# Second chunk's scores issued ahead of its global scores, shifted values behind the casts, first FFN steps interleaved by tile

## The chip, the cores and the metric

The kernel runs on one NeuronCore of a Trainium2 chip. A core has five engines with a queue each, worked off in order: TensorE (PE, matrix products; PEld is its weight load), VectorE (DVE), ScalarE (ACT), GpSimd (POOL) and SyncE (SP), which here only issues DMAs. TensorE writes to PSUM, eight banks of 2 KB in each of 128 partitions; VectorE and ScalarE read it from there. Semaphores make an engine wait for another. The metric is the device time of one execution in microseconds, lower is better.

## What is computed

Sparse attention over 8 batches, 8 heads, 576 positions and 64 dimensions, with a window of 32 to each side and 8 global positions, followed by a gated feed-forward block (FFN):

```python
mask = np.abs(pos[:, None] - pos[None, :]) <= window
mask = mask | is_global[:, None] | is_global[None, :]
attn = softmax(np.where(mask, scale * q @ k.T, -1e9))
x = (attn @ v).transpose(0, 2, 1, 3).reshape(4608, 512)
g, val = x @ w_gate, x @ w_val
ffn_out = (gelu(g) * val) @ w_out
out = x + sigmoid(x @ w_res) * ffn_out
```

Inputs and output are float32; the products run in bfloat16. q, k and v are random, the global positions are drawn at random too.

## The kernel before, in words

The 4608 tokens are worked in nine chunks of 512, each of eight windows of 64 tokens (a batch has nine windows). A chunk goes through attention and then through the FFN: twelve steps `ffn_in` (two products of 512 columns, g_ps and v_ps; Gelu on ScalarE; a product on VectorE into ht) and four times `ffn_out`, one for each tile of 128 tokens: a gate (r_ps, then tanh into rsb) and three thirds of four matmuls into f_ps, the last followed by prb on VectorE, ob on GpSimd and the store on SP's queue. The order of all instructions is written out by hand: each engine gets them in the order of the program, and the loop puts the attention of chunk c + 1 between the gates and thirds of chunk c.

Attention of a chunk has these pieces. `scores(c, quad)` makes the windowed scores of four windows in four PSUM banks, called sc: heads 0 to 3 (pp = 0) in two banks of the pool pss, heads 4 to 7 (pp = 1) in two of the pool psm; for the second chunk ScalarE's exp is written back to the bank, and the returned `mask` multiplies it by maskw on VectorE into pt. `global_scores(b)` makes the global rows and columns of batch b: sg, 288 columns in each of the two banks of the pool psn, and ss, 320 columns in a bank of pss. `global_exp` (L481) takes the exp of both, into ptg and gt, and multiplies gt by maskr on VectorE. `global_rows` (L488) makes the values of the global rows, sn, and vgs from it. `local_values` (L551) and `values` (L567) then make the attention output of one tile of 128 tokens in two banks, nd: 16 products with pt, two or four with gt and vgs, then rden and xtok on VectorE. `turn_x` (L591) transposes xtok on TensorE (tx) and copies it to xt, the operand of the FFN.

PSUM pools are rings: psm has four banks (g_ps, v_ps, r_ps, f_ps, half of sc), pss two (the other half of sc, ss, transposes), psn one pair (sg, nd, from the third batch on also sn). A new tile waits until the one that had its place has been read.

Values are held twice: ve for windows that start at an even multiple of 64, vo shifted by half a tile for odd ones. For batch 1, the casts from float32 to ve and the copies from ve to vo (`shift_on_chip`, L106, two copies for each n) are on GpSimd, in its queue between the casts of the staged weight pieces (L145), which come over SP's queue. Chunk 1 has windows 8 of batch 0 and 0 to 6 of batch 1, so its tiles 1, 2 and 3 read vo at n = 0, 1 and 2.

The first chunk's FFN is begun tile by tile: `begin(t)` (L756) issues the four products of steps j = 0 and 1 for the 128 tokens of tile t. The place between the first chunk's FFN and the second chunk's attention is written out on its own, at L852 to L893.

Of the kernel before, what the change touches and what calls it, by code (L numbers as in the profile page):

```python
# [8 lines left out]
F32 = mybir.dt.float32  # L9
# [3 lines left out]
ACTF = mybir.ActivationFunctionType  # L13
# [10 lines left out]
def kernel(  # L24
# [12 lines left out]
    nc = tc.nc  # L37
# [4 lines left out]
    SCALE = 1.0 / float(D) ** 0.5  # L42
# [15 lines left out]
    psm = ctx.enter_context(tc.tile_pool(name="psm", bufs=4, space=bass.MemoryType.PSUM))  # L58
# [44 lines left out]
        eng.dma_start(vo[b % 2][0:64, 0:4, :, :], ve[b % 2][64:128, 0:4, :, :])  # L103
        eng.dma_start(vo[b % 2][64:128, 0:4, :, :], ve[b % 2][0:64, 1:5, :, :])

    def shift_on_chip(n):  # L106
        nc.gpsimd.tensor_copy(vo[1][64:128, n:n + 1, :, :], ve[1][0:64, n + 1:n + 2, :, :])
        nc.gpsimd.tensor_copy(vo[1][0:64, n:n + 1, :, :], ve[1][64:128, n:n + 1, :, :])


    def flat32(t, o):
# [356 lines left out]
    def global_scores(b):  # L468
        sg = psn.tile([128, 2, 512], F32, name="sg", tag="nd")
        for hf in range(2):  # L470
            for p in range(NP):
                nc.tensor.matmul(sg[32 * p:32 * p + 32, hf, 0:288], kgz[b % 2][:, p, :],  # L472
                                 qt[b % 2][:, p, 288 * hf:288 * hf + 288], start=True, stop=True)
        ss = pss.tile([128, 5, 64], F32, name="ss", tag="sc")
        for c in range(5):
            for p in range(NP):
                nc.tensor.matmul(ss[:, c, 16 * p:16 * p + 16], kt[b % 2][:, p, 128 * c:128 * c + 128],  # L477
                                 qgz[b % 2][:, p, :], start=True, stop=True)
        return sg, ss

    def global_exp(b, sg, ss):  # L481
        e = b % 2
        nc.scalar.activation(ptg[e], ss, ACTF.Exp, bias=0.0, scale=SCALE)
        g = gt[e][:, 64:64 + S]
        nc.scalar.activation(g.rearrange("p (a c) -> p a c", a=2), sg[:, :, 0:288], ACTF.Exp, bias=0.0, scale=SCALE)
        nc.vector.tensor_tensor(g, g, maskr, ALU.mult)

    def global_rows(b):  # L488

        e = b % 2  # L490
        if b > 1:
            sn = psn.tile([128, 2, 512], F32, name="sn", tag="nd")[:, 0, 0:2 * VG]
        else:
            sn = pss.tile([128, 2 * VG], F32, name="sn", tag="sc")
        for c in range(-1, 5):
            for p in range(NP):
                if c < 0:
                    nc.tensor.matmul(sn[32 * p:32 * p + 32, :], own[e][:, 32 * p:32 * p + 32],
                                     view(vgb, 0, 128, (b // 2) * VG, [[0, 2], [1, VG]]), start=True, stop=False)
                else:  # L500
                    nc.tensor.matmul(sn[32 * p:32 * p + 16, :], ptg[e][:, c, 16 * p:16 * p + 16],
                                     ve[e][:, c, 2 * p:2 * p + 2, :], start=False, stop=(c == 4))
        nc.vector.tensor_tensor(view(vgs, 0, 128, e * H * VG, [[2 * VG, NP], [VG, 2], [1, VG]]),
                                view(sn, 0, 128, 0, [[0, NP], [VG, 2], [1, VG]]),
                                view(head8, 0, 128, 0, [[2, NP], [1, 2], [0, VG]]), ALU.mult)
# [24 lines left out]
        nc.scalar.activation(sc if stay else mine, sc, ACTF.Exp, bias=0.0, scale=SCALE)  # L530
        return mine, sc if stay else mine

    def scores(c, quad):

        i0 = (CH * c + 4 * quad) % NW
        banks = []
        for pp, pool, tag in ((0, pss, "sc"), (1, psm, "mm")):
            sc = [pool.tile([128, 2, 4, 64], F32, name="sc", tag=tag) for _ in range(2)]
            heads(c, quad, pp, sc, True)
            banks += [(pp, u, sc[u]) for u in range(2)]  # L540
        mine = [weigh(quad, *which, stay=(c == 1)) for which in banks]

        def mask(n0, n1):
            for m, x in mine[n0:n1]:
                nc.vector.tensor_tensor(m, x, view(maskw, 0, 128, 64 * i0, [[0, 2], [64, 4], [1, 64]]), ALU.mult)  # L545
        return mask
# [206 lines left out]
    values(0, 1, begun_v[1])  # L753
    begun = [ffn_steps(0, j) for j in range(2)]

    def begin(t):  # L756
        for steps in begun:
            for what in "gv":
                steps[what](128 * t, 128 * t + 128)

    values(0, 2)
    turn_x(0, 0)
    begin(0)
    values(0, 3)
    turn_x(0, 1)
    begin(1)
    turn_x(0, 2)
    turn_x(0, 3)
    begin(2)
    begin(3)  # L770
# [8 lines left out]
    for c in range(NCH):  # L779
# [8 lines left out]
        for j in range(NFF):  # L788
            if c or j > 1:
                ffn_in(c, j, turns.get(j) if c == 0 else None)  # L790
            if c == 0:
                if j == 0:
                    mask_rows(0, NW)
                elif j == 1:
                    mask_rows(NW, NWM)
                    zero_k(1)
                elif j == 2:
                    zero_gt(1, nc.vector)
                    zero_globals(1)
                    for n in range(1, B // 2):  # L800
                        nc.vector.tensor_single_scalar(idx[:, n:n + 1], idx[:, 0:1], float(2 * H * S * n), ALU.add)
                elif j == 3:
                    zero_v(1, nc.vector)
                elif j == 4:
                    double_qk(0, 1)
                elif j == 6:
                    got = turn_globals(0, 1)
                    for what in "kq":
                        DVE(compact[what][:, 0:1, :], got[what])
                    spread_qk(1, compact, 0, {"k": DVE, "q": ACT})  # L810
                elif j == 5:
                    for p in (0, 1, 2, 3, -1):
                        for what in "kq":
                            cast_pair(1, p, what, POOL)
                    load_vraw(1)
                    for n in (14, 15):
                        load_piece(n)
                    for n in (12, 13):
                        cast_piece(n, POOL)
                    for n in range(16, 20):  # L820
                        load_piece(n)
                    for c5 in range(5):
                        cast_v(1, c5, POOL)
                        if c5 in (1, 2):
                            shift_on_chip(c5 - 1)
                    for n in range(14, 20):
                        cast_piece(n, POOL)
                        if n == 15:
                            shift_on_chip(2)
                    shift_on_chip(3)  # L830
                if j == 10:
                    turn(3)
            elif b < B:
                if c % 2 == 1:
                    n0, n1 = b // 2, b // 2 + 1
                    if j == 8:
                        double_qk(n0, n1)
                    elif j == 9:
                        got = turn_globals(n0, n1)
                        for what in "kq":  # L840
                            DVE(compact[what][:, n0:n1, :], got[what])
                        spread_v(n0, n1)
                if j == 8:
                    shift_v(b)
                    if b + 1 < B:
                        load_qk(b + 1)
                if j == 9:
                    spread_qk(b, compact, (b // 2) * 128, {"k": DVE, "q": DVE})
                if j == 11:
                    held = global_scores(b)  # L850
        work_f = [w for t in range(4) for w in ffn_out(c, t)]
        if c == 0:  # L852
            def third(t, n):
                work_f[4 * t + 1 + n]()

            global_exp(1, *global_scores(1))
            work_f[0]()
            scores(1, 0)(0, 4)
            work_f[4]()
            work_f[8]()  # L860
            mask = scores(1, 1)
            mask(0, 2)
            work_f[12]()
            global_rows(1)
            mask(2, 4)
            for what in "kq":
                load_second(what)
            cast_second("k", 0, NQT, ACT)
            began = local_values(1, 0)
            third(0, 0)  # L870
            values(1, 0, began)
            third(1, 0)
            values(1, 1)
            third(2, 0)
            turn_x(1, 0)
            third(3, 0)
            values(1, 2)
            turn_x(1, 1)
            third(0, 1)
            cast_second("q", 0, 1, POOL)  # L880
            values(1, 3)
            third(1, 1)
            cast_second("q", 1, 3, POOL)
            turn_x(1, 2)
            third(2, 1)
            third(3, 1)
            turn_x(1, 3)
            for t in range(4):
                third(t, 2)
                if t == 1:  # L890
                    cast_second("q", 3, NQT, POOL)
                    turn_qk(2, "k")
            continue  # L893
# [50 lines left out]
```

## Time and profile before

| | us |
|---|---|
| median of 4 runs | 397.74 |
| lowest and highest | 396.79, 398.22 |
| the profiled execution | 398.05 |
| its span | 396.3 |
| TensorE busy | 380.6 |
| VectorE busy | 203.8 |
| GpSimd busy | 170.9 |
| ScalarE busy | 168.2 |
| TensorE busy from 23.00 to 31.35 us (8.35) | 6.27 |
| TensorE busy from 51.31 to 65.09 us (13.78) | 12.40 |

The span is the time from the first to the last instruction of the program in the trace; the profiled execution's own time holds what lies around it too. Times of events below are counted from the span's start. [...]two neighbours overlap by about 0.16 us, and a group of four with 512 columns, shown as 1.02 to 1.04 us, is followed by the next after 0.86. The granted TensorE clock was 1.00 throughout.

### The profile page before, as it was taken

Reading aid. Unit: us, or ns where it says so; the run is one execution under the profiler, and the core shown is the slowest. Engines: PE = TensorE matmul, PEld = TensorE weight load, DVE = VectorE, ACT = ScalarE, POOL = GpSimd, SP = SyncE. Lnnn points to the kernel's source line nnn. Section 1 sums busy time; section 2 is a strip of 40 time slices with the busy share of each in tenths; the row PEclk is TensorE's granted clock in tenths of the full one; section 3 lists DMA queues with packets and bytes.
Section 4 is the critical chain, followed back from the end, with each engine's and each line's share of the span. In section 5 each row is a group of like instructions: output and inputs, shape, how many; then the busy total and the mean of one; then the engine's idle time right before and its main releaser. Section 6 shows DMA issues by size and latency. Waiting matters only on the chain.

```text
span 396.3 us, 8484 instructions
## 1 busy us (share of the span) xinstructions
PE 380.6 (96%) x3360; PEld 197.1 (50%) x3360; DVE 203.8 (51%) x445; ACT 168.2 (42%) x279; POOL 170.9 (43%) x207
## 2 busy tenths in 40 slices
PE   3979989999999999999999999999999999999996
PEld 2665546444554454445544554455445544554444
DVE  7766676446733464456444554565345633463423
ACT  5653585136333542355334623373336333633321
POOL 7977794768247614471395226612501110021012
PEclk9999999999999999999999999999999999999999
DMA  8999999399939962999299949993990310051002
GB/s 249 268 379 348 231 348 195 97 164 171 97 108 144 190 70 80 127 197 101 79 132 158 140 82 108 184 101 84 116 152 19 94 55 0 2 92 57 0 29 79
DMA packets 153002, 52.78 MB, mean 133 GB/s; under 512 B 136386, under 2 KB 143426, under 8 KB 152962
## 3 DMA queue, kind: packets, MB, share of 16 engines
q1 hardware_dynamic: 77024, 41.88, 46.1%
q0 software_dynamic: 75392, 9.84, 41.4%
q8 instruction: 26, 0.43, 0.5%
q10 hardware_dynamic: 546, 0.52, 0.4%
q14 instruction: 14, 0.11, 0.1%
HBM read 39.19 MB, written 9.44 MB: 123 GB/s over the span
## 4 chain that ended last, share of the span: by engine, by line
PE 85%; DVE 5%; DMA 3%; ACT 2%; issue 2%; POOL 2%; DVEq 0%; POOLq 0%
PE f_ps L661 21%; PE g_ps L618 21%; PE v_ps L618 21%; PE r_ps L636 7%; PE nd L563 4%; PE sc L523 3%; PE nd L575 2%; DMA kt<-k_st 2%; DMA vgf<-in_v_dram,idx 1%; PE ss L477 1%; POOL ve L99 1%; DVE pt L545 1%; PE sg L472 1%; PE sc L512 1%; PE tx L598 1%
## 5 line engine op out<-in xcount | busy, mean ns | idle before, releaser
L625 DVE SCALAR_TENSOR_TENSOR ht<-gsb,v_ps 128x512 bf16<-128x512 bf16 x108 | 74.1, 687 | 98.9 <-PE v_ps L618 91.5
L624 ACT ACTIVATE gsb<-g_ps 128x512 bf16<-128x512 f32 x108 | 64.4, 597 | 126.3 <-PE g_ps L618 126.3
L667 POOL TENSOR_TENSOR ob<-prb,xtok 128x512 f32<-128x512 f32 x35 | 40.3, 1155 | 175.8 <-DVE prb L665 175.8
L618 PE MATMUL g_ps<-xt,wg_t 128*128 128x512 bf16 (+1 forms) x456 | 111.9, 368 | 1.8 <-ACT xt L599 1.8
L618 PE MATMUL v_ps<-xt,wv_t 128*128 128x512 bf16 (+1 forms) x456 | 111.9, 368 | 0.1
L661 PE MATMUL f_ps<-wo_t,ht 128*128 128x512 bf16 x420 | 100.4, 379 | 0.0
L618 PEld LDWEIGHTS <-wg_t 128*128 128x128 bf16 x456 | 43.4, 98 | 51.2 <-issue 2.9
L618 PEld LDWEIGHTS <-wv_t 128*128 128x128 bf16 x456 | 43.4, 98 | 49.4 <-DVE xtok L582 0.3
L661 PEld LDWEIGHTS <-ht 128*128 128x128 bf16 x420 | 38.8, 97 | 38.5
L639 ACT ACTIVATE rsb<-r_ps 128x512 bf16<-128x512 f32 x36 | 21.6, 604 | 71.0 <-PE r_ps L636 71.0
L665 DVE SCALAR_TENSOR_TENSOR prb<-rsb,f_ps 128x512 f32<-128x512 bf16 x35 | 24.0, 685 | 27.4 <-PE f_ps L661 26.4
L636 PE MATMUL r_ps<-wr_t,xt 128*128 128x512 bf16 x144 | 36.8, 379 | 0.0
L530 ACT ACTIVATE pt<-sc 128x512 bf16<-128x512 f32 x64 | 33.3, 614 | 5.2 <-PE sc L523 5.2
L91 POOL DMA_DIRECT2D q_st<-in_q_dram x25 | 21.4, 865 | 21.1 <-DMA qt<-q_st 21.0
L545 DVE TENSOR_TENSOR pt<-pt,maskw 128x512 bf16<-128x512 bf16 x56 | 23.2, 424 | 7.8 <-ACT pt L530 5.8
L563 PEld LDWEIGHTS <-pt 128*128 128x128 bf16 x576 | 21.9, 97 | 8.5 <-DVE xtok L588 1.2
L99 POOL DMA_DIRECT2D ve<-in_v_dram x30 | 25.5, 864 | 0.0
L588 DVE TENSOR_TENSOR xtok<-nd,rden 128x512 bf16<-128x512 f32 x34 | 23.5, 691 | 1.3
L91 POOL DMA_DIRECT2D k_st<-in_k_dram x25 | 21.1, 868 | 4.0 <-DMA kt<-k_st 2.3
L587 DVE RECIPROCAL rden<-nd 128x8 f32<-128x8 f32 x34 | 7.1, 207 | 30.4 <-PE nd L575 30.3
L563 PE MATMUL nd<-ve,pt 128*128 128x65 bf16 x320 | 22.5, 193 | 0.0
L636 PEld LDWEIGHTS <-xt 128*128 128x128 bf16 x144 | 13.4, 97 | 15.0
(168 smaller groups left out, 308.7 us busy)
## 6 DMA issues: line engine op xcount, KB each, us to landing
out_dram<-ob SPq DMA_DIRECT2D x35, 256.0 KB, 2.2
vo<-ve SPq DMA_DIRECT2D x12, 260.0 KB, 5.8
q_st<-in_q_dram POOLq DMA_DIRECT2D x20, 128.0 KB, 6.1
k_st<-in_k_dram POOLq DMA_DIRECT2D x20, 128.0 KB, 6.3
ve<-in_v_dram POOLq DMA_DIRECT2D x18, 128.0 KB, 6.9
wo_t<-in_k_dram SPq DMA_DIRECT2D x8, 256.0 KB, 6.2
vraw<-in_q_dram SPq DMA_DIRECT2D x8, 256.0 KB, 7.5
extra<-in_moe_w_out_dram SPq DMA_DIRECT2D x4, 512.0 KB, 7.3
```

The lines of the kernel that those rows point to most:

```text
L91: nc.gpsimd.dma_start(dst[0:n, r, :].rearrange("p (h d) -> p h d", d=D), src[b].rearrange("h s d -> s h d")[128 * r:128 * r + n])
L99: nc.gpsimd.dma_start(t[p0:p1, c, :, 0:D], v[b].rearrange("h s d -> s h d")[s0 + p0:s0 + p1])
L530: nc.scalar.activation(sc if stay else mine, sc, ACTF.Exp, bias=0.0, scale=SCALE)
L545: nc.vector.tensor_tensor(m, x, view(maskw, 0, 128, 64 * i0, [[0, 2], [64, 4], [1, 64]]), ALU.mult)
L563: nc.tensor.matmul(nds[h // 4][:, VG * (h % 4):VG * (h % 4) + VG], view(pt, 0, 128, c0, [[1, 128]]), vw, start=(h % 4 == 0 and e == 0), st ...
L618: nc.tensor.matmul(held[what][:, c0:c1], w[:, kk, 128 * j:128 * j + 128], x[:, kk, c0:c1], start=(kk == 0), stop=(kk == NKT - 1))
L624: nc.scalar.activation(gsb, held["g"], ACTF.Gelu, bias=0.0, scale=1.0)
L625: nc.vector.scalar_tensor_tensor(ht[:, j, :], gsb, 0.5, held["v"], ALU.mult, ALU.mult)
L636: nc.tensor.matmul(r_ps, xt[c % 2][:, kk, 128 * t:128 * t + 128], wr_t[:, kk, :], start=(kk == 0), stop=(kk == NKT - 1))
L661: nc.tensor.matmul(held["f"], ht[:, j, 128 * t:128 * t + 128], wo_t[:, j, :], start=(j == 0), stop=(j == NFF - 1))
L665: nc.vector.scalar_tensor_tensor(prb, held["r"], 1.0, held["f"], ALU.add, ALU.mult)
L667: nc.gpsimd.tensor_tensor(ob, prb, xtok[c % 2][:, t, :], ALU.add)
```

## The change

Four things are changed. The first steps of the FFN are put in another order among the attention tiles and transposes. For the second chunk, the scores of heads 0 to 3 are issued before the global scores, and the masks are split in the same way; ss goes into the columns of sg's two banks that are free (288 to 480 of the first, 288 to 416 of the second), so that its exp is two instructions; sn takes psn's pair for batch 1 as well. The value products of the second chunk's first tile follow vgs and stand ahead of the first third. And the four shifts of batch 1's values stand behind its casts: n = 0 on GpSimd behind the last v cast, n = 3 behind the last weight cast, n = 1 and 2 on ScalarE behind the last gate.

```diff
-    def shift_on_chip(n):
-        nc.gpsimd.tensor_copy(vo[1][64:128, n:n + 1, :, :], ve[1][0:64, n + 1:n + 2, :, :])
-        nc.gpsimd.tensor_copy(vo[1][0:64, n:n + 1, :, :], ve[1][64:128, n:n + 1, :, :])
+    def shift_on_chip(n, copy):
+        copy(vo[1][64:128, n:n + 1, :, :], ve[1][0:64, n + 1:n + 2, :, :])
+        copy(vo[1][0:64, n:n + 1, :, :], ve[1][64:128, n:n + 1, :, :])
...
-        ss = pss.tile([128, 5, 64], F32, name="ss", tag="sc")
+        if b == 1:
+            ss = [sg[:, c // 3, 288 + 64 * (c % 3):352 + 64 * (c % 3)] for c in range(5)]
+        else:
+            ss_all = pss.tile([128, 5, 64], F32, name="ss", tag="sc")
+            ss = [ss_all[:, c, :] for c in range(5)]
...
     def global_exp(b, sg, ss):
         e = b % 2
-        nc.scalar.activation(ptg[e], ss, ACTF.Exp, bias=0.0, scale=SCALE)
+        to = ptg[e].rearrange("k c r -> k (c r)")
+        done = 0
+        for part in ss:
+            n = part.shape[1]
+            nc.scalar.activation(to[:, done:done + n], part, ACTF.Exp, bias=0.0, scale=SCALE)
+            done += n
...
     def global_rows(b):
...
-        if b > 1:
+        if b:
             sn = psn.tile([128, 2, 512], F32, name="sn", tag="nd")[:, 0, 0:2 * VG]
...
-    def scores(c, quad):
+    def scores(c, quad, pps=(0, 1)):
...
-        for pp, pool, tag in ((0, pss, "sc"), (1, psm, "mm")):
+        for pp in pps:
+            pool, tag = (psm, "mm") if pp else (pss, "sc")
...
-    def begin(t):
-        for steps in begun:
+    def begin(t, js=(0, 1)):
+        for j in js:
             for what in "gv":
-                steps[what](128 * t, 128 * t + 128)
+                begun[j][what](128 * t, 128 * t + 128)
 
     values(0, 2)
     turn_x(0, 0)
-    begin(0)
     values(0, 3)
     turn_x(0, 1)
+    begin(0, (0,))
+    turn_x(0, 2)
+    begin(0, (1,))
     begin(1)
-    turn_x(0, 2)
     turn_x(0, 3)
     begin(2)
     begin(3)
...
                     for c5 in range(5):
                         cast_v(1, c5, POOL)
-                        if c5 in (1, 2):
-                            shift_on_chip(c5 - 1)
+                    shift_on_chip(0, POOL)
                     for n in range(14, 20):
                         cast_piece(n, POOL)
-                        if n == 15:
-                            shift_on_chip(2)
-                    shift_on_chip(3)
+                    shift_on_chip(3, POOL)
...
-            global_exp(1, *global_scores(1))
+            scores(1, 0, (0,))(0, 2)
+            got = global_scores(1)
+            scores(1, 0, (1,))(0, 2)
+            global_exp(1, *got)
             work_f[0]()
-            scores(1, 0)(0, 4)
             work_f[4]()
+            scores(1, 1, (0,))(0, 2)
             work_f[8]()
-            mask = scores(1, 1)
-            mask(0, 2)
+            mask = scores(1, 1, (1,))
             work_f[12]()
             global_rows(1)
-            mask(2, 4)
+            mask(0, 2)
+            for n in (1, 2):
+                shift_on_chip(n, ACT)
             for what in "kq":
                 load_second(what)
             cast_second("k", 0, NQT, ACT)
-            began = local_values(1, 0)
+            values(1, 0)
             third(0, 0)
-            values(1, 0, began)
+            values(1, 1)
             third(1, 0)
-            values(1, 1)
             third(2, 0)
```

`work_f` holds the gates at 0, 4, 8 and 12 and the thirds between them; `third(t, n)` issues third n of tile t.

More of the change, by code (lines that the diff above doesn't have):

```diff
@@ L473, in global_scores @@
                                  qt[b % 2][:, p, 288 * hf:288 * hf + 288], start=True, stop=True)
-        ss = pss.tile([128, 5, 64], F32, name="ss", tag="sc")
+        if b == 1:
[3 more added lines that the diff above has]
+            ss = [ss_all[:, c, :] for c in range(5)]
         for c in range(5):
             for p in range(NP):
-                nc.tensor.matmul(ss[:, c, 16 * p:16 * p + 16], kt[b % 2][:, p, 128 * c:128 * c + 128],
+                nc.tensor.matmul(ss[c][:, 16 * p:16 * p + 16], kt[b % 2][:, p, 128 * c:128 * c + 128],
                                  qgz[b % 2][:, p, :], start=True, stop=True)
-        return sg, ss
+        return sg, [sg[:, 0, 288:480], sg[:, 1, 288:416]] if b == 1 else [ss_all.rearrange("k c r -> k (c r)")]
     def global_exp(b, sg, ss):
         e = b % 2
-        nc.scalar.activation(ptg[e], ss, ACTF.Exp, bias=0.0, scale=SCALE)
+        to = ptg[e].rearrange("k c r -> k (c r)")
[4 more added lines that the diff above has]
+            done += n
         g = gt[e][:, 64:64 + S]
```

## The prediction

> **What bounds the kernel now.** I read the page first (busy shares and the chain that ended last), then TensorE's timeline where the chain leaves TensorE, then VectorE's and ScalarE's timelines there, last the DMA landings that feed GpSimd.
>
> ```profile
> PE 380.6 (96%) x3360; PEld 197.1 (50%) x3360; DVE 203.8 (51%) x445; ACT 168.2 (42%) x279; POOL 170.9 (43%) x207
> PE 85%; DVE 5%; DMA 3%; ACT 2%; issue 2%; POOL 2%; DVEq 0%; POOLq 0%
> ```
>
> TensorE is the bound: time can be won only where it stands. From 75 to 380 us it hardly does (windows: 20.00 busy of 20.00, 20.00 of 20.00, 264.20 of 265.00). The change touches two stretches before that. The first, at 23 to 31 us, starts the FFN tile by tile (TensorE's timeline: start, duration, line, work, idle before and its releaser):
>
> ```profile
> 23.10 0.69 PE L598 MATMUL tx<-ident,xtok 128*128 128x128 bf16 x4
> 24.46 0.38 PE L618 MATMUL g_ps<-xt,wg_t 128*128 128x128 bf16 x4 [0.67 <-ACT xt L599]
> 25.44 0.40 PE L618 MATMUL v_ps<-xt,wv_t 128*128 128x128 bf16 x4
> 26.38 0.38 PE L598 MATMUL tx<-ident,xtok 128*128 128x128 bf16 x4
> 27.44 0.38 PE L618 MATMUL g_ps<-xt,wg_t 128*128 128x128 bf16 x4 [0.67 <-ACT xt L599]
> 28.33 0.61 PE L598 MATMUL tx<-ident,xtok 128*128 128x128 bf16 x8
> 29.39 0.38 PE L618 MATMUL g_ps<-xt,wg_t 128*128 128x128 bf16 x4 [0.45 <-ACT xt L599]
> 31.35 1.02 PE L618 MATMUL g_ps<-xt,wg_t 128*128 128x512 bf16 x4
> ```
>
> Each turn (tx) is followed at once by the product that needs its copy, so TensorE waits for the copy three times. The second, 51.3 to 65.1 us, goes from the first chunk's FFN to the second chunk's attention (TensorE, then VectorE, then ScalarE):
>
> ```profile
> 53.72 0.62 PE L523 MATMUL sc<-qt,kt 64*128 64x64 bf16 x31 [0.38 <-ACT ptg L483]
> 56.97 0.42 PE L523 MATMUL sc<-qt,kt 64*128 64x64 bf16 x16 [0.41 <-DVE pt L545]
> 59.87 1.02 PE L661 MATMUL f_ps<-wo_t,ht 128*128 128x512 bf16 x4
> 62.42 0.20 PE L563 MATMUL nd<-vo,pt 128*128 128x65 bf16 x1 [0.22 <-DVE xtok L588]
> ```
>
> ```profile
> 54.24 1.48 DVE L486 TENSOR_TENSOR gt<-gt,maskr 128x576 bf16<-128x576 bf16 x1 [1.60 <-ACT gt L485]
> 55.64 3.81 DVE L545 TENSOR_TENSOR pt<-sc,maskw 128x512 bf16<-128x512 f32 x6
> 59.49 0.70 DVE L503 TENSOR_TENSOR vgs<-sn,head 128x520 bf16<-128x520 f32 x1
> 60.10 1.28 DVE L545 TENSOR_TENSOR pt<-sc,maskw 128x512 bf16<-128x512 f32 x2
> ```
>
> ```profile
> 51.94 1.28 ACT L483 ACT_TABLE_LOAD   x1
> 54.57 2.08 ACT L530 ACTIVATE sc<-sc 128x512 f32<-128x512 f32 x4
> ```
>
> VectorE has no gap from 54.24 to 62.36, ScalarE none from 51.3 to 60.1; TensorE's work in these 13.78 us, at its own pitches (four full 512-column matmuls 0.864, 16 score matmuls 0.29, a value tile 0.49), is 11.45, so it loses 2.3.
>
> [...] The trace shows 1.28 and the exp directly behind it (53.23)[...]; I take 1.28. [...] the gt product took 1.48 beside GpSimd's casts, and 0.46 at 97.34 us, when GpSimd only issued DMAs.
>
> **Part 1, first steps interleaved (gain).** The new order is turn 0, values tile 3, turn 1, steps of tile 0 for j=0, turn 2, those for j=1, tile 1, turn 3, tiles 2 and 3. Work is the same; I walk it with the trace's times. Turn 0's last matmuls go at 23.5 and it ends issuing at 23.7. Values tile 3 uses the pair of banks that tile 1 frees when VectorE's xtok ends at 24.29: start 24.35, 0.49 + 0.22, end 25.06. Turn 1 to 25.28. j=0 for tile 0 (copy ready 24.42) 0.44, to 25.72. Turn 2 (xtok ends 25.38) to 25.94. j=1 0.44, to 26.38 (its bank, free at 25.38, no longer stops it). Tile 1 (ScalarE's copy 25.5 to 26.1) 0.89, to 27.28. Turn 3 (xtok for tile 3: VectorE free at 25.38, 0.2 + 0.7, ends 26.3) to 27.50. Tile 2 (copy 26.1 to 26.7) to 28.39, tile 3 (VectorE's copy ends 28.1) to 29.28. Before it was 31.17 (30.95 + 0.22). Gain 1.89, between 1.5 (a copy late once more, 0.4) and 2.0 (all the idle there is). Cover lost: none; the FFN steps behind it need weight casts that end at 24.9 (j=2, needed at 29.5), 30.3 (j=4, needed 33) and 35.8 (j=8, needed 40).
>
> **Part 2, scores first, shared banks (cost).** Times of the trace before, moved by nothing; part 1 is subtracted at the end. TensorE: first two score banks 51.4 to 51.7 (the slots come free at 50.93 and 51.30 with the kt and qt copies), sg and ss to 52.6, two more score banks to 52.9, first two gates to 54.65. ScalarE loads its table as before, 51.94 to 53.22; the load now carries waits for TensorE and VectorE, both over by 51.9. Then four exps at 0.49, to 55.2; two ptg parts of 192 and 128 columns instead of one of 320 (0.44)[...]; gt exp to 56.2; two gates to 57.2; exps of the second half to 58.1; gate; exps to 59.55; last gate 60.1. VectorE: four masks at 0.635 from 53.78 to 56.3; gt product to 57.8 if blocked like before, 56.8 if not; I take blocked, though it matters little, since mask five needs ScalarE at 57.6; masks five and six to 59.0; vgs to 59.7; the last two masks to 60.9; rden and xtok to 61.9, against 62.36 before. TensorE waits 0.4 for the third pair of score banks, 0.35 for gate three, 0.2 and 0.2 after (banks held by masks and gates); then sn 58.3 to 58.7. Now the loss: sn, sg and the value tiles share one pair of banks. The first value tile cannot start until vgs has read sn, 59.77: 1.03 idle, where before the tile ran early and the first output third (0.86) lay behind it. Then tile 0 to 60.71, third to 61.57, tile 1 waits for xtok until 61.94 and ends 62.65; thirds 1, 2, turn, third 3 (2.80) end at 65.46. Before: 65.09. So VectorE's 0.45 is won and 0.86 of work is put behind it: cost 0.37. Bounds: gain 0.5 if the gt product is short and banks come free a little earlier[...].
>
> **Part 3, shifted values (nothing).** GpSimd loses four copies (0.65 each, 2.6) ahead of its last v cast, but that cast's data lands at 51.14 (landings from the DMA issues), so it ends near 51.8 instead of 53.45; sn needs it at 58.3 - 1.89 = 56.4, and did not wait before. The out weights land at 52.36 to 60.42; the last cast ends near 61.6 as before, the thirds that need it start near 69. ScalarE's four copies (1.06 for twice the size at 20.8 us; 0.55 each) run at 60.1 to 62.3, on the shifted clock 58.2 to 60.4; behind them in its queue are the k_st casts, whose data lands at 61.5 to 65.8. The DMAs on SP's queue (second k and q loads) hang on the same casts and stay. GpSimd's q casts stand ahead of the first outputs: the third q row lands at 69.33, its cast ends 70.0, the first output now comes at 71.1. TensorE would be held there only from a shift of about 3.5. Price if the cover failed: 0.4, the copy that values tile 2 needs.
>
> **Sum.** -1.89 + 0.37 = -1.52. The profiled execution took 398.05 (span 396.3), so 396.5; the median of the runs, 397.74, is 0.3 below it, so 396.2.
>
> **Rivals.** (B) The second stretch gains too: banks freed earlier because masks start at 53.78 instead of 55.64, gt product short, so -0.5 there: -2.4, 395.3. For: VectorE idles 1.6 before its gt product now. Against: ScalarE has no gap, and the last exps cannot come earlier. (C) The shared pair costs more than worked: vgs 1.0 later, so -0.5, 397.2. For: it hangs on ScalarE's order (gates ahead of exps five and six)[...]. Against: each hand-over was timed above. (D) Slower: [...] the product beside a later cast of GpSimd (up to 1.04 more); TensorE has nothing in front of the first value tile, so each microsecond on vgs is one on the end. It decides from vgs later than 61.2 (1.52 beyond 59.7)[...]. For: no cover is left. [...]
>
> **How the numbers follow.** A 0.50 (its own range 395.5 to 396.9), B 0.18, C 0.23, D 0.09. A measurement of this kernel tells 0.3% (1.2 us) from no change. Faster by more: 0.8 of A, all of B, a little of C: 0.60. Slower: most of D, 0.08. Within: 0.32. The range takes in B and most of C: 394.9 to 397.6.
>
> **What would show it.** Right: the first 512-column g_ps starts near 29.5; idle before the first value tile of the second chunk near 1 us, released by vgs; all later stages the same length. Wrong: first g_ps after 30; that value tile released otherwise; idle between 65 and 95 us, where nothing is foreseen.

## The result and the profile after

The changed kernel took 396.66 us (median of 42 runs, 395.28 to 400.56), the kernel before 397.73 (63 runs, 395.96 to 400.58): 1.07 us less, a ratio of 0.9971 with a 95% interval of 0.9961 to 0.9981. The profiled execution took 395.56 us, its span is 393.9. That is 2.4 us under the span before, more than the medians differ, because one execution also carries chance: in this one the first transpose of the first chunk came at 22.17 us instead of 23.10, from code that the change leaves alone, and over the fourteen profiles of this study it came anywhere from 22.07 to 23.28.

The page's first part, busy time by engine:

```profile
PE 379.9 (96%) x3360; PEld 196.8 (50%) x3360; DVE 202.3 (51%) x445; ACT 170.7 (43%) x284; POOL 168.6 (43%) x203
```

TensorE is as busy as before. ScalarE's busy time rose by 2.5 us, for four copies of GpSimd's and one more exp, and GpSimd's fell by 2.3. The first stretch in TensorE's timeline (start, duration, line, work):

```profile
22.17 0.68 PE L608 MATMUL tx<-ident,xtok 128*128 128x128 bf16 x4
23.40 0.20 PE L573 MATMUL nd<-ve,pt 128*128 128x65 bf16 x1 [0.55 <-DVE xtok L598]
24.12 0.38 PE L608 MATMUL tx<-ident,xtok 128*128 128x128 bf16 x4
24.34 0.39 PE L628 MATMUL g_ps<-xt,wg_t 128*128 128x128 bf16 x4
24.79 0.39 PE L608 MATMUL tx<-ident,xtok 128*128 128x128 bf16 x4
26.35 0.39 PE L608 MATMUL tx<-ident,xtok 128*128 128x128 bf16 x4
28.54 1.02 PE L628 MATMUL g_ps<-xt,wg_t 128*128 128x512 bf16 x4
```

No transpose and no step waits for a copy any more: none of their lines has a bracket. What is left is 0.55 us in front of the values of tile 3, which VectorE's xtok releases (the working had about 0.65). The second stretch, TensorE, VectorE and ScalarE:

```profile
52.55 0.39 PE L532 MATMUL sc<-qt,kt 64*128 64x64 bf16 x15 [0.36 <-DVE pt L555]
53.14 1.02 PE L646 MATMUL r_ps<-wr_t,xt 128*128 128x512 bf16 x4 [0.21 <-DVE pt L555]
57.04 0.64 PE L573 MATMUL nd<-ve,pt 128*128 128x65 bf16 x16 [0.94 <-DVE vgs L512]
59.21 0.20 PE L573 MATMUL nd<-vo,pt 128*128 128x65 bf16 x1 [0.22 <-DVE xtok L598]
```

```profile
51.20 2.48 DVE L555 TENSOR_TENSOR pt<-sc,maskw 128x512 bf16<-128x512 f32 x4 [1.38 <-ACT sc L539]
53.62 0.46 DVE L495 TENSOR_TENSOR gt<-gt,maskr 128x576 bf16<-128x576 bf16 x1
55.09 1.29 DVE L555 TENSOR_TENSOR pt<-sc,maskw 128x512 bf16<-128x512 f32 x2 [1.01 <-ACT sc L539]
56.30 0.69 DVE L512 TENSOR_TENSOR vgs<-sn,head 128x520 bf16<-128x520 f32 x1
```

```profile
49.30 1.28 ACT L539 ACT_TABLE_LOAD   x1 [0.18 <-issue]
50.59 2.05 ACT L539 ACTIVATE sc<-sc 128x512 f32<-128x512 f32 x4
```

The first four masks do start ahead of the gt product, but the third pair waits 1.01 us for ScalarE, and TensorE stands 0.94 us in front of the second chunk's first value tile until vgs is made. The gt product took 0.46 us instead of 1.48.

Lengths of TensorE's stages, from the starts of its matmuls in the profiles, in us. "First steps" is from the first tx to the first 512-column g_ps; "transition" from the last matmul of the first chunk's last v_ps to the first third of its fourth tile; "thirds" from there to the second chunk's first g_ps; "two steps" from there to the v_ps of its third step.

| profile | first steps | transition | thirds | two steps |
|---|---|---|---|---|
| before | 8.25 | 13.23 | 10.03 | 4.32 |
| after | 6.37 | 13.69 | 10.10 | 4.75 |
| difference | -1.88 | +0.46 | +0.07 | +0.43 |

The sum is -0.92. The rest of the distance between the two spans is the earlier start (0.93) and one shorter wait for a transpose of k by DMA later on (0.2 instead of 0.7 us, between 190 and 290 us). Both vary between executions: the wait was anything from none to 0.9 us over the fourteen profiles.

### The profile page after: what moved, and what is told of

Read it like the earlier page. It is cut to its first block, busy times and chain, and to the rows that moved or that the text cites. A ratio compares the mean times of both kernels' runs of the same rounds, so it can differ in the third digit from the quotient of the medians.

```text
span 393.9 us, 8481 instructions
## 1 busy us (share of the span) xinstructions
PE 379.9 (96%) x3360; PEld 196.8 (50%) x3360; DVE 202.3 (51%) x445; ACT 170.7 (43%) x284; POOL 168.6 (43%) x203
## 4 chain that ended last, share of the span: by engine, by line
PE 72%; DMA 16%; SPq 4%; POOL 3%; issue 2%; DVE 1%; ACT 1%; ACTq 0%; DVEq 0%; POOLq 0%
PE f_ps L671 19%; PE v_ps L628 18%; PE g_ps L628 18%; PE r_ps L646 7%; DMA extra<-in_moe_w_val_dram 5%; PE nd L573 3%; DMA extra<-in_moe_w_out_dram 3%; SPq L185 2%; PE sc L532 2%; DMA wo_t<-in_k_dram 2%; PE nd L585 2%; DMA kt<-k_st 2%; DMA xtok<-in_v_dram 2%; DMA vgf<-in_v_dram,idx 1%; DMA ht<-in_q_dram 1%
```

## The experiments

The theory after the result was that the first steps give 1.9 us, that scores first takes back 0.4 to 0.5 because TensorE has no work left ahead of the first value tile, and that the start of the second chunk's FFN takes a little more. The rivals were: the steps give only what the total shows and all else is neutral; or the loss lies in VectorE's chain, or in the shared banks as such.

**The order of the first steps alone**, in the kernel before:

```diff
     turn_x(0, 0)
-    begin(0)
     values(0, 3)
     turn_x(0, 1)
+    begin(0, (0,))
+    turn_x(0, 2)
+    begin(0, (1,))
     begin(1)
-    turn_x(0, 2)
...
```

> The kernel before with the new order of the first FFN steps alone. My theory (the steps give 1.9 us and the other parts take some of it back): from turn 0 to the first 512-column g_ps 6.4 us instead of 8.25, the transition unchanged at 12.9 us from the end of v_ps to the fourth first third, total 1.5 to 1.9 us faster than before (ratio about 0.9957). Rival (the steps give only about the whole measured 1.1 us, all else is neutral): ratio about 0.9971, and at least 0.7 us of the won time stands idle again before 50 us.

First steps 6.38, transition 13.23, thirds 10.03, two steps 4.32: only the first stage moved, by 1.87. The time was 395.81 against 398.32, ratio 0.9939 [0.9920, 0.9958]. The rival's 0.9971 is outside. The 2.5 us between the medians are more than the stage gives: the kernel before was slow in this timing, whose 398.32 lies 0.6 to 0.8 above its median in the other four (397.57 to 397.73).

**All the rest alone**, the changed kernel with the old `begin`:

```diff
     turn_x(0, 0)
+    begin(0)
     values(0, 3)
     turn_x(0, 1)
-    begin(0, (0,))
+    begin(1)
     turn_x(0, 2)
-    begin(0, (1,))
-    begin(1)
     turn_x(0, 3)
...
```

> The changed kernel with the old order of the first FFN steps, so scores first, shared banks and moved shifts alone. My theory: 0.4 us slower than before (ratio 1.001), with about 0.9 us idle before the second chunk's first value tile, released by vgs. Rival B (scores first gains): 0.5 us faster, ratio 0.9987. Rival (neutral): 1.000.

Transition 13.69, thirds 10.10, the 0.94 us idle as foreseen, but the time was 398.14 against 398.32, ratio 0.9991 [0.9977, 1.0004]: the stages say 0.5 slower (1.0012 to 1.0013), and this interval leaves that out. It was timed again beside the kernel before against itself:

> The kernel before, unaltered, timed against itself, to see how far a ratio of this kernel moves by itself and for a second profile of it. Both theories: ratio 1.000 within 0.0015; its stages as in the first profile (8.25 us for the first steps, 13.23 for the transition).

> Scores first, shared banks and moved shifts alone, once more. By the sum of its stages it should be 0.5 us slower than before (ratio 1.0013), while its first timing gave 0.9991 with an interval that leaves this out. My theory (the first timing's runs of before were slow by accident): 1.000 to 1.002. Rival (the parts gain something that one profile's stages do not show): below 0.9995 again.

The kernel before against itself gave 0.9993 [0.9968, 1.0018], so a ratio moves by 0.0007 with nothing changed. The rest alone gave 1.0001 [0.9985, 1.0016], 0.6 us to either side: the 0.37 us of the working and the 0.46 of the stages both lie inside. In this second timing, where the kernel before was not slow, the runs neither show nor exclude them. The traces do show a longer transition, 13.69 in both profiles of this kernel, but the kernel before is not steady there either. VectorE in its second profile, and GpSimd beside it:

```profile
53.95 1.88 DVE L486 TENSOR_TENSOR gt<-gt,maskr 128x576 bf16<-128x576 bf16 x1 [1.60 <-ACT gt L485]
55.76 3.67 DVE L545 TENSOR_TENSOR pt<-sc,maskw 128x512 bf16<-128x512 f32 x6
```

```profile
52.95 0.61 POOL L190 CAST ve<-wo_t 96x512 bf16<-96x512 f32 x1
53.50 2.02 POOL L145 CAST wo_t<-extra 128x1024 bf16<-128x1024 f32 x2
```

The product took 1.88 us this time and the transition 13.57 (from 50.71 to 64.28). The kernel with the first steps alone is a third sample of the old order in this place. VectorE in its profile:

```profile
51.93 0.67 DVE L486 TENSOR_TENSOR gt<-gt,maskr 128x576 bf16<-128x576 bf16 x1 [1.60 <-ACT gt L485]
52.91 2.48 DVE L545 TENSOR_TENSOR pt<-sc,maskw 128x512 bf16<-128x512 f32 x4 [0.31 <-ACT sc L530]
```

Here the product took 0.67 us and the transition was 13.23, as with 1.48: the masks behind a short product wait for ScalarE (0.31 us). Counted from the last matmul of v_ps, vgs started at 8.48 after 0.67, at 8.49 after 1.48 and at 8.84 after 1.88. So even at the head of VectorE's masks a product of up to about 1.5 us costs nothing, and only what it takes beyond that goes into the chain (an estimate from these three). The second profile of before thus explains 0.34 of the 0.46; against the other two samples the rest alone stays 0.46 longer.

**Thirds ahead of the value tiles**, in the changed kernel:

```diff
-            values(1, 0)
             third(0, 0)
-            values(1, 1)
+            values(1, 0)
             third(1, 0)
+            values(1, 1)
```

> The changed kernel with the first third of tile 0 ahead of the second chunk's first value tile, and that of tile 1 ahead of the second. My theory (TensorE has no cover while vgs is made): the idle 0.94 us before the value tile goes to about 0.1, the fourth first third comes 0.7 to 0.9 us earlier, total up to 0.8 us faster than the changed kernel, less what GpSimd's q casts take at the start of the second chunk's FFN. Rival (the loss is in VectorE's chain whatever TensorE does): the idle time only moves ahead of the second value tile, total the same as the changed kernel.

Transition 12.83, 0.86 less than in the changed kernel, exactly one third (four matmuls at 0.216 us). The wait in front of the value tile is gone and the one in front of the second tile, 0.22 us, did not grow, so the time did not move there; the rival falls. The time was 395.89 against 398.32, ratio 0.9947 [0.9928, 0.9967], with six runs and without the changed kernel beside it.

**sn in a bank of its own**, and the value products of the first tile ahead of the first third, as before:

```diff
-        if b:
+        if b > 1:
...
-            values(1, 0)
+            began = local_values(1, 0)
             third(0, 0)
-            values(1, 1)
+            values(1, 0, began)
             third(1, 0)
+            values(1, 1)
```

> The changed kernel with sn back in a bank of its own pool and the value products of the first tile ahead of the first third, as before. My theory (only the work that stands ahead of vgs's release counts, not the pair of banks as such): the transition takes 12.8 us to the fourth first third, as with the thirds first, so 0.86 us less than in the changed kernel. Rival (taking the banks apart brings its own wait, because sn must wait for a bank that mask five frees): 0.2 us or less is won.

Transition 12.96, with 0.20 us in front of sn for the bank that a mask frees. So 0.73 of the 0.86 are won: the shared pair is not dear in itself, the missing cover (work of TensorE that could run while vgs is made) is. The time was 395.41 against 397.66, ratio 0.9925 [0.9897, 0.9953].

**q casts behind the first outputs.** The 0.43 us in "two steps" of the profile after are two waits, of 0.19 and 0.25 us, for f_ps banks: prb waits for a buffer that ob on GpSimd frees, and GpSimd had to cast the third q row first, which had landed at 71.27 us (its landing before: 69.33). GpSimd in the profile after:

```profile
71.39 0.61 POOL L205 CAST q_st<-vraw 128x512 bf16<-128x512 f32 x1 [0.51 <-PE f_ps L671]
71.97 2.26 POOL L677 TENSOR_TENSOR ob<-prb,xtok 128x512 f32<-128x512 f32 x2
```

```diff
-            cast_second("q", 1, 3, POOL)
...
-                    cast_second("q", 3, NQT, POOL)
+                    cast_second("q", 1, NQT, POOL)
```

> The changed kernel with GpSimd's casts of the second and third q row moved behind its first two outputs. My theory (the earlier TensorE meets q rows whose landing did not move: 0.43 us of waits in the first two FFN steps of the second chunk): these waits go, 0.3 to 0.5 us faster than the changed kernel. Rival (those waits were an accident of one execution, or the later steps have slack for them): same time, and the waits of 0.2 us each are absent in the changed kernel's other runs too, which the idle time there in this call's other profiles would show.

The waits are gone (4.32), but they are absent in all the other profiles too, those without this edit among them; the rival was right that one execution made them. The time was 396.02 against 398.32, ratio 0.9949 [0.9932, 0.9966].

**The changed kernel again, and thirds first with the q casts later**, timed together with sn apart and the shifts back:

> The changed kernel unaltered, as the measure for the runs beside it. My theory: the first steps are 1.87 us shorter than before, the transition 0.46 longer, so about 1.4 us faster than before where the third q row lands by about 70.4 us, and 1.0 where it lands at 71.3, with waits of about 0.2 us twice in the second chunk's first two FFN steps. Rival (those waits are part of every execution): 1.0 us faster and the waits are there whatever the landing.

> The changed kernel with the thirds of tiles 0 and 1 ahead of the value tiles and the q casts behind the first two outputs. My theory: the fourth first third comes 0.86 us earlier counted from the end of the FFN steps, no wait at the start of the second chunk's FFN whatever the landing, together 0.9 to 1.3 us faster than the changed kernel beside it, about 2.3 faster than before. Rival (what is won ahead of 75 us waits for DMAs later): no more than 0.4 us faster than the changed kernel.

The changed kernel: stages 6.38, 13.69, 10.10 and 4.32 with the third q row landed at 70.36, as the theory had it. The time was 396.34 against 397.66, ratio 0.9956 [0.9940, 0.9973]. Both edits together had a transition of 12.82 and two steps of 4.32, at 395.53, ratio 0.9924 [0.9898, 0.9950]. That is 0.8 us under the changed kernel by the medians beside it, a little short of the 0.9 to 1.3 expected and about what the third is worth by its stage, so the later casts add nothing that shows.

**The shifts back on GpSimd**, the changed kernel otherwise, timed twice:

```diff
-                    shift_on_chip(0, POOL)
+                        if c5 in (1, 2):
+                            shift_on_chip(c5 - 1, POOL)
...
+                        if n == 15:
+                            shift_on_chip(2, POOL)
...
-            for n in (1, 2):
-                shift_on_chip(n, ACT)
```

> The changed kernel with all four shifts on GpSimd in their old places. My theory (the shifts are worth nothing): all stages of TensorE within 0.1 us of the changed kernel, total the same. Rival (the shifts off GpSimd bring the v casts of batch 1 in time): sn waits for the last v cast, up to 0.5 us slower than the changed kernel.

> The kernel with all shifts back on GpSimd once more, as the measure for the run beside it. My theory (with the shifts in GpSimd's queue its casts stand back to back, and the gt product, which reads two SBUF operands, waits for up to two of them): the gt product takes 1.3 to 2.8 us, where the changed kernel had 0.46, and the transition is 14.0 to 14.9 us. Rival (the 2.73 us were an accident of one execution): 0.5 us and 13.7.

By the medians nothing changed (396.25 beside 396.34 for the changed kernel; ratios 0.9961 [0.9944, 0.9977] and 0.9963 [0.9946, 0.9980]). But the first profile, of the slowest of its 17 runs (397.62), was not within the 0.1 us expected: it had a transition of 14.86 and TensorE idle for 2.12 us in front of the value tile. VectorE, then GpSimd, in that profile:

```profile
54.15 2.73 DVE L495 TENSOR_TENSOR gt<-gt,maskr 128x576 bf16<-128x576 bf16 x1
56.80 1.28 DVE L555 TENSOR_TENSOR pt<-sc,maskw 128x512 bf16<-128x512 f32 x2
```

```profile
53.99 0.61 POOL L190 CAST ve<-wo_t 96x512 bf16<-96x512 f32 x1
54.55 2.02 POOL L145 CAST wo_t<-extra 128x1024 bf16<-128x1024 f32 x2
56.63 0.72 POOL L107 COPY vo<-ve 64x520 bf16<-64x520 bf16 x1
```

sn did not wait for the v casts (it came at 56.10, right behind the gate), so the rival is not it. The product ends at 56.88, 0.31 us after GpSimd's unbroken run of casts ends at 56.57. In the second profile it took 1.70 us and ended 0.31 us after the run of casts that ended at 55.43; in the two profiles of before it ended 0.31 us after 55.41 and after 55.52. The transition with 1.70 was 13.82, less than the 14.0 to 14.9 expected: here too the third pair of masks waits for ScalarE anyway. Counted from the last matmul of v_ps, vgs started at 8.11 after products of 0.46 to 1.24 us, at 8.25 after 1.70 and at 9.28 after 2.73, so about 1.56 us are free in this order (an estimate from these).

With the shifts moved the product took 0.46 to 1.24 us over eight profiles, always within what is free; with the shifts in their old place, and both operands in SBUF, it took 0.67, 1.48, 1.70, 1.88 and 2.73. A run of casts does not always hold it up to its end. The product, and the second of two casts beside it, in the profile with the q casts later:

```profile
53.77 0.83 DVE L495 TENSOR_TENSOR gt<-gt,maskr 128x576 bf16<-128x576 bf16 x1
```

```profile
54.24 1.27 POOL L145 CAST wo_t<-extra 128x1024 bf16<-128x1024 f32 x1
```

The first of these casts ended at 54.29. The product ended 0.31 us after that, and the second cast, begun behind the first without a pause, took 1.27 us instead of 1.04. With sn apart the product took 0.79 us. Why it ended there, and in the four profiles above only behind the run of casts, stays open.

**The product with one operand in SBUF**, with the shifts back as well: the exp of batch 1's rows is written back to PSUM and read there.

```diff
+        g2 = g.rearrange("p (a c) -> p a c", a=2)
+        got = sg[:, :, 0:288] if b == 1 else g2
+        nc.scalar.activation(got, sg[:, :, 0:288], ACTF.Exp, bias=0.0, scale=SCALE)
...
+            nc.vector.tensor_tensor(g2, got, maskr.rearrange("p (a c) -> p a c", a=2), ALU.mult)
```

> The same kernel with the exp of batch 1's global rows written back to its PSUM banks and the gt product reading it there, so that one of its operands only is in SBUF. My theory (it is the second SBUF operand that makes it wait for GpSimd): the product takes 0.7 to 0.8 us beside the same casts, mask five starts within 0.1 us of its exp, and the transition is 13.7 us. Rival (VectorE is slowed beside GpSimd's casts whatever it reads, or the product waits for data): 1.3 us or more, as without the edit.

VectorE and GpSimd in it:

```profile
54.38 0.76 DVE L498 TENSOR_TENSOR gt<-sg,maskr 128x576 bf16<-128x576 f32 x1
55.86 1.29 DVE L560 TENSOR_TENSOR pt<-sc,maskw 128x512 bf16<-128x512 f32 x2 [0.73 <-ACT sc L544]
```

```profile
53.74 2.02 POOL L145 CAST wo_t<-extra 128x1024 bf16<-128x1024 f32 x2
```

The product took 0.76 us in the middle of the same two casts, though they leave no pause, where with both operands in SBUF it took 2.73 and 1.70: in these profiles the wait comes with the second operand in SBUF. The masks, which read one operand from PSUM, agree: four of them took 2.48 or 2.49 us in every profile of the changed order, whatever GpSimd did beside them. Mask five waits for its exp again (0.73 us). The transition was 13.83, since ScalarE's exp into PSUM began 0.2 us later, so the edit wins nothing by itself. The time was 396.35 against 397.69, ratio 0.9968 [0.9943, 0.9992].

## Why the prediction was right

396.2 was forecast, 396.66 measured, inside the range; faster, by 1.07 us in the first timing and 1.3 by the medians of the second (1.7 by its ratio), where 1.5 was forecast. That is near the bound of what a measurement can tell: 1.07 lies within the 1.2 us that the prediction counted as no change, which it gave 0.32, while it gave 0.60 to more.

**Part 1** was worked out to -1.89 and measured as -1.86 to -1.88 in every profile that has it, alone or with the rest. Walking the queues with the trace's own times was enough, since what each wait hung on, a copy or an xtok, stood in the trace with its start and duration. The 0.18 us in front of the first 512-column group, which waits for Gelu, moved along unchanged.

**Part 2** was put at +0.37, and the profiles give +0.46: TensorE idle in front of the value tile was 1.03 in the working and 0.94 on the chip, the released bank waits came as 0.36 and 0.21. Two terms were off. The table load stood 0.18 us behind Gelu's end, for which the trace names no releaser, where before it followed at once; I had it at nothing. And the product was taken as blocked, 1.48, and took 0.46; as the working said, this hardly mattered, for mask five waits for ScalarE. What the working missed is that the kernel *before* is not steady in this place: its transition was 13.23 in two samples and 13.57 in a third, where the product took 1.88. The 0.37 is thus borne out by the stages of the traces, against the usual sample of the old order. By the time of whole runs it is not shown: the rest alone came within 0.6 us of before to either side.

The table load itself took 1.28 us, as in the working, and the exp starts 0.01 us behind its end, before (51.94 and 53.23) as after (49.30 and 50.59). The two parts of ptg took 0.54 us together, where one exp of 320 columns took 0.44. Rival D needed vgs more than 1.52 us late, and of this the product beside a later cast was given 1.04 at most; the rest was the author's estimate, which no trace shows. In the new order a product that delays vgs by more than 0.2 us is seen in one execution, with the shifts back: it took 2.73 us with both operands in SBUF, and vgs started 1.17 us later than after a short one (9.28 against 8.11). With one of its operands in PSUM it took 0.76 beside such casts.

**Part 3** was put at nothing, which by the medians it is, but the reasons were incomplete. Not only must sn find its v casts done: the place of the shifts among the casts also bears on how long VectorE's product waits, and the execution with 2.73 us shows what moving the shifts protects against. And the move has a small price: "thirds" took 10.10 or 10.11 us in all eight profiles with the shifts moved and 10.02 or 10.03 in the six with the shifts in their old place. In the same part the q rows were taken to be safe up to a shift of 3.5 us, from one landing at 69.33; over the profiles that show it the landing came from 68.97 to 71.75, and at 71.27 TensorE lost 0.43 at a shift of 2.3. That is idle time between 65 and 95 us, which the prediction had named as a sign of being wrong; waits of that size came in one profile of fourteen.

Rival B found no support: no profile of the changed kernel shows a gain in the second stretch. Rival C named a vgs that comes 1.0 us late; in the profile after, vgs ended 8.79 us behind the last matmul of v_ps, where the working had 8.77, so C's late vgs is not seen there either, only in the execution with 2.73 us. That the first timing, 1.07, lies about midway between A's 1.5 and C's 0.5 does not speak for C.

**Versions that beat before by more** are the changed kernel with thirds first and the q casts later, or with sn apart: 0.8 and 0.9 us below the changed kernel timed beside them, 2.1 and 2.3 below before, with eight or nine runs each. Most of this needs only the first part of the change: with the new order of the first steps alone the kernel took 395.81, beside 395.89 for thirds first and 396.02 for the q casts later in the same timing. The rest of the change as it stands adds nothing that shows.

## What to carry to other kernels

Where one engine is busy 96% of the time, list its waits with their releasers, and ask of each move what stands in front of the next wait as cover: here one reorder removed three waits for a copy, and another ate part of the gain because it removed the work standing ahead of vgs. Where a block of matmuls depends on nothing that is still to come, as the first thirds here, try it ahead of the first instruction that needs a hand-over: that moved 0.86 us. Time the parts of a change alone as well: here one of them gave all the gain that shows. Take landings of DMAs from more than one execution before calling a transfer hidden, and give the kernel before a second profile too, since its stages can vary as much as the change is worth.

## What was not expected of the hardware

A VectorE product of two bf16 operands in SBUF, 0.46 us while GpSimd only issued DMAs (before, at 97.34 us), took up to 2.73 us beside GpSimd's casts. In eight profiles in which it took longer than 0.46 us (0.62, 0.67, 0.83, 0.84, 1.48, 1.70, 1.88 and 2.73) it ended 0.30 or 0.31 us after the end of one of GpSimd's casts or copies. In four of them the product had first stood through one or two changes from one cast to the next that left no pause (the next begins about 0.05 us before the end of the last); in one, with 0.83, it ended 0.31 us after such a change, and the cast behind it took 0.23 us longer. What decides between the two is not shown. With one of its operands in PSUM the product took 0.76 us in the middle of such casts (one profile).
